# A planned single-core kernel (Fourier mixing beside 16-head attention): the planner's margin behind some loads is 3 instead of 5

## Chip, cores, metric

One core of one Trainium2 chip. The time is the device time of one execution in microseconds (us), the median over several runs.

## What is computed

Two independent layers on 2048 tokens of width 448, joined along the last axis. In float32 throughout:

```python
# A: Fourier mixing with given matrices
a = x @ dft_hid_re.T
b = x @ dft_hid_im.T
yA = dft_seq_re @ a - dft_seq_im @ b
# B: full softmax attention, 16 heads of 28
q, k, v = split(xB @ wqkv)
p = softmax(q @ k.T * 28**-0.5)
yB = (p @ v).reshape(2048, 448) @ wo
out = concat([yA, yB], axis=-1)
```

## The kernel before

**Attention** fills most of the time. Scores are made transposed, 128 keys by 512 queries at a time: per head 16 key tiles times 4 query chunks, 1024 tiles in all. Each is one matmul on PE (L1302; L1243 for a head's first key tile) into a bank, then an exponential on ACT (L1310) into a buffer `kept`; every four matmuls of a key tile (L1285) then add values weighted by these into one bank per head. There are eight banks: one for filler work, seven for scores and sums. A head's first key tile goes a longer way: ACT copies it out (L1247), DVE transposes it and takes maxima (L1248, L1249, L1255, L1260, L1258), spreads the result over the query columns (transpose L1269), POOL or DVE puts it in as one more row of that head's queries (L1272), and adds it to the copied tile (L1274), which ACT exponentiates (L1276). No other score matmul of the head can start before its L1272.

**Fillers** are PE work that stands between the score matmuls: projections to queries, keys and values (L687, 512 or 224 columns) and the Fourier side (L877). A projection from column block 3 on needs a *weight piece*: 256 KB loaded on SP (L612) into a buffer `raw`, converted on ACT (L613) and its rest made on POOL (L616).

**Checks.** The Fourier side does not multiply by the whole 2048 x 2048 matrices. It uses their symmetries and checks them on all entries: pieces of both matrices go through six buffers `raw` (loads L928 and, of a mirrored copy, L966), are added or subtracted (L972, on DVE or POOL, whichever is free) and reduced to a maximum on DVE (L909). Token pieces (L821, L824) and folded weights (L584 to L587, converted on ACT at L589) use the same buffers.

**What sets the order.** Every engine has its own instruction order, and all of them come from a planner that runs when the kernel is built (`Schedule.run`, L237 on). It takes tasks with guessed durations, dependencies and due times (`key`) and plays the five engines forward in time: when an engine is free, it gets the ready task that is due first, and a task with a choice of engines goes to whichever of them comes first. The order in which tasks are handed out becomes the order of instructions; on the chip each instruction waits by semaphores for what it really needs. For a load the planner guesses a landing from a flow of 225 GB/s and a fixed time, and then adds the task's `slack` before it lets a consumer start:

```python
lat = max(landed[-len(t.dmas):]) - at + 0.1 + t.slack
```

`slack=SLACK` stands at the loads of matrix entries (`Stack.loads` L928, `Turned` L966, `Rows` L1045, `column_check` L1020, two loads in `special`), of token pieces (L821, L824), of folded weights (L584, L587) and of weight pieces (L612). Loads of keys and queries (L1181, L1182) have a margin of their own, `SLACK_K`, which is 2.5.

Of the kernel before, what the change touches and what calls it, by code (L numbers as in the profile page):

```python
# [36 lines left out]
LEAD = 6  # L37
NFILL = 1
V_OWN = 2
SLACK = 5.0  # L40
MIRROR_AT = 60.0, 110.0
FILL_AT = 48.0, 75.0
N_WARM = 9
# [311 lines left out]
def tile_kernel(ctx, tc, xa, wre, wim, wd, xb, wqkv, wo, out):  # L355
# [82 lines left out]
    def dma(key, emit, size=256, extra=0.0, n=1, **kw):  # L438

        return sch.add({"SP": 0.4}, key, lambda e: emit(), dmas=[(size, extra)] * n, **kw)  # L440
# [5 lines left out]
    def act(key, emit, d=ACT_P, **kw):  # L446
        return sch.add({"ACT": d}, key, lambda e: emit(), **kw)
# [4 lines left out]
    def pool(key, emit, d=POOL_2, **kw):  # L452
        return sch.add({"POOL": d}, key, lambda e: emit(), **kw)
# [125 lines left out]
    def load_folded(part, key, after):  # L579
# [3 lines left out]
        cols = slice(part * D, (part + 1) * D)  # L583
        lw = [dma(key, lambda: nc.sync.dma_start(w()[:, :, :E], wd[:, :2, part * D:part * D + E]), 226, slack=SLACK, use=[raws[2]])]  # L584
        ld = dma(key + 0.5, lambda: nc.sync.dma_start(n()[:, :, :D], wd[:, :2, cols]), 448, acq=[raws[0]])
        ld2 = dma(key + 0.7, lambda: nc.sync.dma_start(n2()[:, :, :D], wd[:, 2:, cols]), 448, acq=[raws[1]])
        ld3 = [dma(key + 1, lambda: nc.sync.dma_start(r()[:, :, :E], wt_d[:, :, part * D:part * D + E]), 226, slack=SLACK, deps=turned[0], use=[raws[3]])]  # L587
        f = lambda l: w_first.folded[:, part, :, l, :]
# [17 lines left out]
    class Piece:  # L606


        def __init__(self, src, key):
            self.hi, self.lo = whi.slot(), wlo.slot()  # L610
            raw = Square(raw_s.slot())
            ld = dma(key, lambda: nc.sync.dma_start(raw.t, src()), 256, slack=SLACK, acq=[raw])  # L612
            a = act(key + 1, lambda: nc.scalar.activation(self.hi.t, raw.t, AF.Copy), ACT_S, soon=SOON,  # L613
# [199 lines left out]
    def tokens(c, key, after):  # L813
# [6 lines left out]
        for q, st in enumerate((c, NH - 1 - c)):  # L820
            ln.append(dma(key + 0.3 * q, lambda q=q, st=st: nc.sync.dma_start(  # L821
                n.t[:, q].rearrange("p (b x) -> p b x", b=2), bass.AP(tensor=xa.tensor, offset=xa.offset + st * tile_x,
                ap=[[4 * P, P], [NH * tile_x, 2], [1, 2 * P]])), 256, slack=SLACK, use=[n]))
            lr.append(dma(key + 0.3 * q + 0.1, lambda q=q, st=st: nc.sync.dma_start(  # L824
                r.t[:, q].rearrange("p (b x) -> p b x", b=2), bass.AP(tensor=xt_d.tensor, offset=xt_d.offset + st * tile_x // 2,
                ap=[[2 * P, P], [NH * tile_x // 2, 2], [1, 2 * P]])), 256, slack=SLACK, deps=turned[1], use=[r]))
        z = [pool(key, lambda p=p, k=k: nc.gpsimd.memset(r.t.rearrange("p a (b k m) -> p (a b) k m", b=2, k=2)[p:p + 1, :, k], 0.0), 0.3, deps=lr, use=[r])
# [88 lines left out]
    def begun(key):  # L916
        return [opened[min(max(int((key - begins[0]) / P_H), 0), H - 1)]]

    class Stack:
# [6 lines left out]
        def loads(self, part, key, n, off, step):  # L926
            src, rows = (wre, wim)[part], P // n
            return [dma(key, lambda a=a: nc.sync.dma_start(self.t[a * rows:(a + 1) * rows], bass.AP(  # L928
                tensor=src.tensor, offset=src.offset + off(a), ap=[[step, rows], [1, H1]])), 512 / n, slack=SLACK, deps=begun(key), use=[self.raw]) for a in range(n)]

# [704 lines left out]
```

## Time and profile before

| | before |
|---|---|
| median of 3 runs | 695.8 us (695.61 to 695.81) |
| profiled execution | 693.96 us, its span 692.4 us |
| granted TensorE clock, mean | 0.998 |
| DMA, mean over the span | 190 GB/s |
| exponentials on ACT (L1310) | 960, 506.0 us busy |
| score matmuls (L1302) | 960, 295.7 us busy |
| value sums (L1285) | 2048, 246.2 us busy |

The profile is one execution. PE is TensorE's matmuls, PEld its weight loads, DVE VectorE, ACT ScalarE, POOL GpSimd, SP the engine that issues DMAs. A row of a group gives line, engine, operation, what is written and read, shapes and count, then busy time, mean duration in ns, and the idle time before it with what ended it. A row of the timeline begins with start and duration in us; idle time before it and what ended it stand in square brackets. The busy time of PE is modelled, as matmuls are pipelined.

### The profile page before, as it was taken

Reading aid. Unit: us, or ns where it says so; the run is one execution under the profiler, and the core shown is the slowest. Engines: PE = TensorE matmul, PEld = TensorE weight load, DVE = VectorE, ACT = ScalarE, POOL = GpSimd, SP = SyncE. Lnnn points to the kernel's source line nnn. Section 1 sums busy time; section 2 is a strip of 40 time slices with the busy share of each in tenths; the row PEclk is TensorE's granted clock in tenths of the full one; section 3 lists DMA queues with packets and bytes.
Section 4 is the critical chain, followed back from the end, with each engine's and each line's share of the span. In section 5 each row is a group of like instructions: output and inputs, shape, how many; then the busy total and the mean of one; then the engine's idle time right before and its main releaser. Section 6 shows DMA issues by size and latency. Waiting matters only on the chain. (4 is left out here: it accounts for less than half of the span.)

```text
span 692.4 us, 12770 instructions
## 1 busy us (share of the span) xinstructions
PE 683.0 (99%) x4147; PEld 395.3 (57%) x4147; DVE 491.8 (71%) x857; ACT 607.7 (88%) x1233; POOL 354.8 (51%) x344
## 2 busy tenths in 40 slices
PE   8999999999999999999999999999999999999996
PEld 7897555555555555455455545555555555455786
DVE  6458639587969489698978796989697927531780
ACT  6416999999998999999999999999999999999442
POOL 8504315357545346554735564548778421545660
PEclk9999999999999999999999999999999999999999
DMA  8866789886969888989779898671443311344177
GB/s 302 282 198 208 187 213 233 215 222 209 250 175 249 214 237 236 229 238 232 217 201 248 222 249 225 185 233 59 147 145 99 101 49 52 99 133 137 34 183 243
DMA packets 101808, 131.38 MB, mean 190 GB/s; under 512 B 34231, under 2 KB 64585, under 8 KB 101733
## 3 DMA queue, kind: packets, MB, share of 16 engines
q1 hardware_dynamic: 99685, 128.62, 67.7%
q0 software_dynamic: 2048, 1.86, 1.1%
q8 instruction: 35, 0.57, 0.4%
q14 instruction: 40, 0.33, 0.2%
HBM read 100.28 MB, written 36.88 MB: 198 GB/s over the span
## 5 line engine op out<-in xcount | busy, mean ns | idle before, releaser
L1310 ACT ACTIVATE kept<-bank 128x512 f32<-128x512 f32 x960 | 506.0, 708 | 13.0 <-PE bank L1302 11.9
L1302 PE MATMUL bank<-q,k 98*128 98x512 f32 x960 | 295.7, 410 | 1.5 <-ACT kept L1310 0.8
L1285 PE MATMUL bank<-kept,v 128*32 128x512 f32 x2048 | 246.2, 598 | 0.0
L1302 PEld LDWEIGHTS bank<-q,k 98*128 98x128 f32 x960 | 171.4, 188 | 129.9 <-ACT kept L1310 92.2
L972 POOL TENSOR_TENSOR raw<-raw,raw 128x1024 f32<-128x1024 f32 (+3 forms) x57 | 107.9, 1898 | 72.3 <-DVE raw L972 37.7
L1285 PEld LDWEIGHTS bank<-kept,v 128*32 128x32 f32 x2048 | 53.4, 109 | 116.5 <-issue 110.8
L909 DVE TENSOR_REDUCE far<-raw 128x1 f32<-128x1024 f32 (+3 forms) x78 | 86.0, 1111 | 8.2 <-POOL raw L1086 4.4
L1274 POOL TENSOR_TENSOR kept<-kept,mb 128x512 f32<-128x512 f32 x41 | 58.2, 1427 | 26.5 <-DVE mb L1269 13.9
L1247 ACT ACTIVATE kept<-bank 128x512 f32<-128x512 f32 x64 | 40.3, 693 | 24.7 <-PE bank L1243 21.6
L1272 POOL CAST q<-mb 1x512 fp32r<-1x512 f32 x31 | 24.6, 808 | 69.3 <-DVE mb L1269 49.2
L1248 DVE STREAM_TRANSPOSE mb<-bank 128x512 f32<-128x512 f32 x64 | 43.6, 700 | 20.0 <-PE bank L1243 15.0
L1348 POOL TENSOR_TENSOR kept<-kept 128x512 f32<-128x512 f32 x16 | 20.9, 1304 | 59.9 <-DVE kept L1343 42.7
L1276 ACT ACTIVATE kept<-kept 128x512 f32<-128x512 f32 x64 | 49.4, 783 | 0.0
L687 PE MATMUL bank<-big,whi 128*128 128x512 f32 x132 | 46.8, 396 | 0.0
L687 PE MATMUL bank<-wd,big 128*128 128x224 f32 x288 | 43.9, 274 | 0.4 <-ACT kept L1310 0.3
L687 PEld LDWEIGHTS bank<-wd,big 128*128 128x128 f32 x288 | 40.5, 191 | 4.7 <-issue 0.8
L1269 DVE STREAM_TRANSPOSE mb<-am 128x512 f32<-128x512 f32 x62 | 41.9, 696 | 0.8
L1249 DVE TENSOR_REDUCE qm<-mb 128x16 f32<-128x512 f32 x64 | 41.5, 668 | 0.4
L972 DVE TENSOR_TENSOR raw<-raw,raw 128x1024 f32<-128x1024 f32 (+3 forms) x27 | 34.5, 1281 | 6.5 <-DMA raw<-wre 6.3
L1339 DVE STREAM_TRANSPOSE kept<-kept 128x512 f32<-128x512 f32 x16 | 11.4, 710 | 27.6 <-ACT kept L1337 27.5
L797 DVE COPY kept<-bank 128x224 f32<-128x224 f32 x32 | 12.3, 386 | 24.1 <-PE bank L687 23.8
L1272 DVE CAST q<-mb 1x512 fp32r<-1x512 f32 x31 | 27.9, 902 | 1.0
(181 smaller groups left out, 782.6 us busy)
## 6 DMA issues: line engine op xcount, KB each, us to landing
raw<-wre SPq DMA_DIRECT2D x64, 256.0 KB
raw<-wim SPq DMA_DIRECT2D x64, 256.0 KB
qkd<-kept SPq DMA_DIRECT2D x40, 256.0 KB
k<-qkd SPq DMA_DIRECT2D x64, 112.0 KB
q<-qkd SPq DMA_DIRECT2D x64, 112.0 KB
kept<-xb SPq DMA_DIRECT2D x16, 256.0 KB
vd<-kept SPq DMA_DIRECT2D x8, 512.0 KB
raw<-wre SPq DMA_DIRECT2D x32, 128.0 KB
```

Of the source, the lines that this page charges most:

```text
L687: nc.tensor.matmul(o.t[:, :cols], w(), x(), start=(i == 0), stop=(i == n - 1))
L909: far_done.append(dve(key, lambda: nc.vector.tensor_reduce(far[rows, part, n:n + 1], t(), axis=AX.X if len(t().shape) == 2 else AX.XY, op= ...
L972: return sch.add(d, at, lambda g: eng[g].tensor_tensor(xv(), xv(), yv(), op=op), deps=[*x.ld, *y.ld, *deps], use=[x.raw, y.raw])
L1248: t = dve(key, lambda o=o, tm=tm: nc.vector.transpose(tm.t, o.t), 0.73, deps=[m], acq=[tm], use=[o], lock=[o], own=RAW_S)
L1249: rs.append(dve(key, lambda tm=tm, c=c: nc.vector.tensor_reduce(qm.t[:, 0, c * NT:(c + 1) * NT], tm.t.rearrange("p (j r) -> p j r", r=32), ...
L1269: t = dve(key, lambda mb=mb, c=c: nc.vector.transpose(mb.t, f32(am.t)[:, c * NT:(c + 1) * NT].unsqueeze(2).to_broadcast([P, NT, 32])), 0.7 ...
L1272: row.append(sch.add({"DVE": 0.95, "POOL": 0.8}, key, lambda e, q=q, mb=mb: eng[e].tensor_copy(q.t[96:97, :], mb.t[96:97, :]), deps=[t], u ...
L1274: sh = sch.add({"DVE": 1.15, "POOL": 1.4}, key + (6 if h == 0 else 0), lambda e, s=s, mb=mb: eng[e].tensor_tensor(s.t, s.t, mb.t, op=ALU.add),
L1276: shown.append(act(key, lambda s=s: nc.scalar.activation(s.t, s.t, AF.Exp, scale=SCALE), ACT_S, deps=[sh], use=[s.pair]))
L1285: nc.tensor.matmul(o.t[c * VW:(c + 1) * VW, :], VT[h].t[:, kt // 4, kt % 4, :], tiles[c].t, start=(kt == 0), stop=(kt == NT - 1))
L1302: m = pe(key, lambda e, o=o, q=q, kt=kt: nc.tensor.matmul(o.t, KT[h][kt // 4].t[:KM, kt % 4 * P:(kt % 4 + 1) * P], q.t[:KM, :], start=True ...
L1310: es[h, kt].append(act(key - 20, lambda o=o, p=p: nc.scalar.activation(p.t, o.t, AF.Exp, scale=SCALE), deps=[m], use=[o, p.pair]))
```

## The change

One number: what the planner adds behind the landings of the loads that carry `slack=SLACK`. The loads, the consumers and the waits stay the same; each engine's order is made anew with it.

```diff
 V_OWN = 2
-SLACK = 5.0
+SLACK = 3.0
 MIRROR_AT = 60.0, 110.0
```

The number of instructions on each engine changes hardly, their order in many places. Tasks that may go to DVE or POOL or ACT also change engines: 15 checks of 128x1024 stand on DVE instead of 13 and 17 on POOL instead of 19, 8 of 128x8 on DVE instead of 4 and 8 on POOL instead of 12, and one of the four 128x256 token conversions moves from ACT to DVE. Three places follow (`bank_122` is the filler bank, `raw` the six load buffers).

**The first weight piece, on ACT and SP** (where head 3's scores end and head 4's begin, heads counted from 0). On ACT before, around the fourth exponential L1276 of head 4's first tile:

```order
L1310 ACTIVATE kept_101<-bank_126 128x512
L1310 ACTIVATE kept_101<-bank_129 128x512
L1310 ACTIVATE kept_106<-bank_127 128x512
L1310 ACTIVATE kept_106<-bank_124 128x512
L1276 ACTIVATE kept_109<-kept_109 128x512
L1310 ACTIVATE kept_104<-bank_128 128x512
L613 ACTIVATE whi<-raw_73 128x512
L1310 ACTIVATE kept_104<-bank_125 128x512
```

And now:

```order
L613 ACTIVATE whi<-raw_73 128x512
L1310 ACTIVATE kept_100<-bank_127 128x512
L1310 ACTIVATE kept_100<-bank_126 128x512
L1310 ACTIVATE kept_107<-bank_125 128x512
L1310 ACTIVATE kept_107<-bank_124 128x512
L1310 ACTIVATE kept_103<-bank_123 128x512
L1310 ACTIVATE kept_103<-bank_128 128x512
L1310 ACTIVATE kept_101<-bank_127 128x512
L1310 ACTIVATE kept_101<-bank_126 128x512
L1276 ACTIVATE kept_109<-kept_109 128x512
```

The conversion L613 stood two places behind that L1276 and stands nine places ahead of it; counted from the start of ACT's order it is 10 places earlier. The other three pieces move up by 30, 6 and 6 places, the second folded weight (L589) by 37 and the first by 8. On SP before, around the load of the same piece:

```order
L928 DMA raw_71<-wre 64x1024 x2
L928 DMA raw_75<-wre 64x1024 x2
L1181 DMA k_86<-qkd 56x1x512
L1182 DMA k_86<-qkd 28x512
L928 DMA raw_74<-wre 64x1024 x2
L1181 DMA k_88<-qkd 56x1x512
L1182 DMA k_88<-qkd 28x512
L928 DMA raw_72<-wre 64x1024 x2
L612 DMA raw_73<-wqkv 128x4x128
```

And now:

```order
L928 DMA raw_71<-wre 64x1024 x2
L928 DMA raw_72<-wre 64x1024 x2
L928 DMA raw_75<-wre 64x1024 x2
L928 DMA raw_74<-wre 64x1024 x2
L1181 DMA k_86<-qkd 56x1x512
L1182 DMA k_86<-qkd 28x512
L928 DMA raw_71<-wre 64x1024 x2
L612 DMA raw_73<-wqkv 128x4x128
L1181 DMA k_88<-qkd 56x1x512
```

The piece is issued two DMAs earlier, and now ahead of the key load into `k_88` instead of behind it. The other three move up by 13, 0 and 2 DMAs; ahead of the third, four loads of matrix entries have moved from behind the key load into `k_85` to in front of it.

**A head's query rows, on DVE** (head 3, its last three transposes L1269). Before:

```order
L1269 STREAM_TRANSPOSE mb_117<-am_120 128x512
L1272 CAST q_95<-mb_116 1x512
L1274 TENSOR_TENSOR kept_111<-kept_111,mb_116 128x512
L909 TENSOR_REDUCE far<-raw_71 128x1
L1274 TENSOR_TENSOR kept_111<-kept_111,mb_117 128x512
L1269 STREAM_TRANSPOSE mb_116<-am_120 128x512
L909 TENSOR_REDUCE far<-raw_75 128x1
L1272 CAST q_98<-mb_116 1x512
L909 TENSOR_REDUCE far<-raw_73 128x1
L1274 TENSOR_TENSOR kept_114<-kept_114,mb_116 128x512
L1269 STREAM_TRANSPOSE mb_117<-am_120 128x512
```

And now:

```order
L1269 STREAM_TRANSPOSE mb_117<-am_120 128x512
L909 TENSOR_REDUCE far<-raw_71 128x1
L1272 CAST q_95<-mb_116 1x512
L972 TENSOR_TENSOR raw_75<-raw_75 128x8
L909 TENSOR_REDUCE far<-raw_75 128x1
L1274 TENSOR_TENSOR kept_102<-kept_102,mb_117 128x512
L1269 STREAM_TRANSPOSE mb_116<-am_120 128x512
L1272 CAST q_98<-mb_116 1x512
L909 TENSOR_REDUCE far<-raw_73 128x1
L972 TENSOR_TENSOR raw_70<-raw_70,raw_74 128x512
L1269 STREAM_TRANSPOSE mb_117<-am_120 128x512
```

Two checks L972 have come to DVE here; the second, which reads two loads, stands directly in front of the last transpose. Over the 15 heads from the second on, the checks, Fourier steps and reductions that stand on DVE between a head's first L1248 and its last L1269 are 57 instead of 84.

**Fillers, on PE** (within head 1's scores). Before:

```order
L1302 MATMUL bank_126<-q_95,k_85 128x512
L1302 MATMUL bank_125<-q_96,k_85 128x512
L687 MATMUL bank_122<-wd,big 128x224 x6
L1302 MATMUL bank_128<-q_98,k_85 128x512
L687 MATMUL bank_122<-wd,big 128x224 x3
L1302 MATMUL bank_124<-q_99,k_85 128x512
L687 MATMUL bank_122<-wd,x_69 128x224 x2
L1302 MATMUL bank_126<-q_95,k_85 128x512
L1302 MATMUL bank_127<-q_96,k_85 128x512
L1285 MATMUL bank_123<-kept_108,v_91 32x512 x2
```

And now:

```order
L1302 MATMUL bank_126<-q_95,k_85 128x512
L687 MATMUL bank_122<-wd,big 128x224 x4
L1302 MATMUL bank_125<-q_96,k_85 128x512
L687 MATMUL bank_122<-wd,big 128x224 x2
L1302 MATMUL bank_128<-q_98,k_85 128x512
L1302 MATMUL bank_127<-q_99,k_85 128x512
L1302 MATMUL bank_124<-q_95,k_85 128x512
L687 MATMUL bank_122<-wd,big 128x224 x2
L1302 MATMUL bank_126<-q_96,k_85 128x512
L1285 MATMUL bank_123<-kept_108,v_91 32x512 x2
```

Eleven fillers stood ahead of the value sums (L1285) here, and eight do now; the other three come behind.

## The prediction

> **What bounds the kernel now.** I read the page first (busy times, slices, chain), then the busy times by stage, then who waited for whom, then single rows. The page's own verdict misleads here: its chain of waits ends at one closing output copy and says nothing of the middle, and PE looks full.
>
> ```profile
> PE 683.0 (99%) x4147; PEld 395.3 (57%) x4147; DVE 491.8 (71%) x857; ACT 607.7 (88%) x1233; POOL 354.8 (51%) x344
> ```
>
> By stage (us, then PE, PEld, DVE, ACT and POOL busy), ACT is the engine with no room between 70 and 640 us; only in the last 52 us is it far from full.
>
> ```profile
> 70.00:100.00 30.00, 30.00 (x188) 15.18 (x191) 13.01 (x25) 30.00 (x62) 8.00 (x7) 1.00 0.88 212
> 100.00:600.00 500.00, 498.91 (x3027) 259.64 (x3020) 397.61 (x627) 486.18 (x982) 273.68 (x235) 1.00 0.71 189
> 600.00:640.00 40.00, 39.55 (x257) 21.84 (x261) 9.14 (x22) 38.72 (x86) 17.91 (x26) 1.00 0.46 139
> 640.00:692.40 52.40, 46.81 (x267) 39.98 (x266) 28.30 (x67) 20.06 (x50) 22.59 (x26) 0.98 0.56 152
> ```
>
> That PE is not the bound shows in the waits of 100 to 600 us (total, times, longest). Its weight loads stood 78.4 us behind ACT, which had not yet freed a bank, while ACT stood only 8.9 us behind the score matmuls and 12.6 us in all. The first row is PE's side, the rest are all that ACT has.
>
> ```profile
> PEld bank L1302 <- ACT kept L1310: 78.4, 120, 0.8
> ...
> ACT kept L1310 <- PE bank L1302: 8.9, 18, 1.0
> ACT kept L1247 <- DVE mb L1248: 1.5, 3, 0.9
> ACT kept L1247 <- PE bank L1243: 1.4, 4, 0.5
> ACT kept L709 <- PE bank L687: 0.6, 1, 0.6
> ACT wd L709 <- PE bank L687: 0.2, 1, 0.2
> ```
>
> So the stage lasts as long as ACT's own work (486.2 of 500 us) plus 13.8 us in which it stands. An order that changes nothing in ACT's work can win at most 13.8 us here, and loses whatever it adds to that.
>
> **The change part by part.** SLACK is no work and no wait of the chip. It is what the planner adds to its guess of a landing before it lets a consumer into the order, so every consumer of matrix entries, token pieces and weight pieces may now stand 2 us earlier in its engine's order, and its buffer comes free 2 us earlier. Nothing moves before about 105 us, and in the last 52 us ACT, and PE but for rows that are never reached, keep their order. The terms lie between.
>
> *The checks on DVE and POOL.* With the margin of 5 they did already run into their loads (DVE and POOL against DMA):
>
> ```profile
> DVE raw L972 <- DMA raw<-wre: 6.3, 1, 6.3
> ...
> POOL raw L972 <- DMA raw<-wre: 18.9, 7, 6.0
> POOL raw L972 <- DMA raw<-wim: 9.6, 5, 2.7
> ```
>
> At 2 us less, more of them will stand, and stand longer: 13 waits now, and 2 us on each of, say, twice as many is some 50 us at most, over two engines that have 102 us (DVE) and 226 us (POOL) free between 100 and 600. That is off the path as long as nobody needed by PE or ACT is queued behind; the rival below is the case in which somebody is. By the order, two 128x1024 and four 128x8 checks also go from POOL to DVE. The rows for DVE, then POOL:
>
> ```profile
> L972 DVE TENSOR_TENSOR raw<-raw,raw 128x1024 f32<-128x1024 f32 x16 | 23.7, 1483 | 6.4 <-DMA raw<-wre 6.3
> L972 DVE TENSOR_TENSOR raw<-raw,raw 128x8 f32<-128x8 f32 x3 | 2.3, 754 | 0.0
> L972 DVE TENSOR_TENSOR raw<-raw 128x8 f32<-128x8 f32 x1 | 1.8, 1751 | 0.0
> ...
> L972 POOL TENSOR_TENSOR raw<-raw,raw 128x1024 f32<-128x1024 f32 x24 | 58.8, 2449 | 28.6 <-DMA raw<-wre 15.9 <-DMA raw<-wim 7.4 <-DMA q<-qkd 4.4
> ```
>
> DVE gains 2 x 1.48 + 4 x 0.75 = 6.0 us of work, POOL loses more; on ACT this is 0. The Trainium skill, page "SBUF — State Buffer", section "Who interferes with whom", speaks against such a move: a DVE instruction with two SBUF inputs and a POOL one that reads SBUF lock each other out for a whole instruction. A check of 8 columns that took 1.75 us where its like took 0.75 fits that. By the rule the six could cost up to 6 x 2.45 = 14.7 us on DVE in place of 6.0, still inside its 102 us.
>
> *One conversion leaves ACT.* One of the four 128x256 token conversions moves from ACT to DVE.
>
> ```profile
> L462 ACT ACTIVATE big<-raw 128x256 fp32r<-128x256 f32 x4 | 2.0, 593 | 0.0
> ```
>
> 2.0 us for four is 0.5 us off ACT, and DVE there has room: **-0.5 us**, bounded by 0 and -0.6.
>
> *The weight pieces.* Here a consumer stands in ACT's own queue. Four pieces (256 KB each) are issued at L612 and converted at L613; the rows give each issue and the conversion.
>
> ```profile
> 194.31 0.60 SPq L612 DMA_DIRECT2D raw<-wqkv  x1
> ...
> 279.99 0.60 SPq L612 DMA_DIRECT2D raw<-wqkv  x1
> ...
> 344.54 0.61 SPq L612 DMA_DIRECT2D raw<-wqkv  x1
> ...
> 415.67 0.60 SPq L612 DMA_DIRECT2D raw<-wqkv  x1
> ```
>
> ```profile
> 202.66 0.63 ACT L613 ACTIVATE whi<-raw 128x512 fp32r<-128x512 f32 x1
> ...
> 289.32 0.63 ACT L613 ACTIVATE whi<-raw 128x512 fp32r<-128x512 f32 x1
> ...
> 352.06 0.74 ACT L613 ACTIVATE whi<-raw 128x512 fp32r<-128x512 f32 x1
> ...
> 423.66 0.92 ACT L613 ACTIVATE whi<-raw 128x512 fp32r<-128x512 f32 x1
> ```
>
> How long such a load flies I take from loads of the same size that were waited for: four issues begin at 75.22 us, the last ends at 79.91, and the check that needs them starts at 84.24; four begin at 107.14, and the check that needs the first two starts at 112.43.
>
> ```profile
> 75.22 4.69 SPq L928 DMA_DIRECT2D raw<-wre  x4
> ...
> 84.24 1.23 DVE L972 TENSOR_TENSOR raw<-raw,raw 128x1024 f32<-128x1024 f32 x1 [6.25 <-DMA raw<-wre]
> ...
> 107.14 2.40 SPq L928 DMA_DIRECT2D raw<-wre  x4
> ...
> 112.43 2.39 POOL L972 TENSOR_TENSOR raw<-raw,raw 128x1024 f32<-128x1024 f32 x1 [6.04 <-DMA raw<-wre]
> ```
>
> So between 4.3 and 5.3 us; I take 5. The time from landing to conversion is then 3.3, 4.3, 2.5 and 3.0 us. By the order, the conversions move up 10, 30, 6 and 6 places on ACT. A place is 4.03 / 8 = 0.50 us:
>
> ```profile
> 182.81 4.03 ACT L1310 ACTIVATE kept<-bank 128x512 f32<-128x512 f32 x8 [0.50 <-PE bank L1302]
> ```
>
> That makes 5.0, 15.1, 3.0 and 3.0 us earlier. The issues move up 2, 13, 0 and 2 places on SP, an estimated 1.2, 9.8, 0 and 1.6 us. What is left is -0.5, -1.0, -0.5 and +1.6 us: at worst ACT stands 0.5 + 1.0 + 0.5 = 2.0 us, and with the flight at 5.3 us 2.9 us. On the other side, the first issue now stands ahead of the key load that SP could issue only at 191.51 us,
>
> ```profile
> 191.51 0.88 SPq L1181 DMA_DIRECT2D k<-qkd  x1
> ```
>
> and the third has four matrix loads moved out from between that key load and itself, so both should leave 2 to 3 us sooner than their places say. Then no conversion waits but the second: I take **+0.6 us**, between 0 and +2.9.
>
> *The fills on PE.* Filler matmuls (projections and transform) fall at other places between the score matmuls. At 113.00 us ACT stood 0.86 us because PE had 11 fillers and a run of sums in front of the next scores.
>
> ```profile
> 109.26 0.49 PE L687 MATMUL bank<-wd,big 128*128 128x224 f32 x3
> ...
> 113.00 1.58 ACT L1310 ACTIVATE kept<-bank 128x512 f32<-128x512 f32 x3 [0.86 <-PE bank L1302]
> ```
>
> Now 8 stand there, three fewer at 0.49 / 3 = 0.16 us at the most, so this wait shrinks by up to 0.5 us; but the three come later and may lengthen another. Over the whole stage the count of fillers done at any score matmul stays within about nine small ones of what it was, and back to equal again and again. A place redrawn gains or loses at random: I take **-0.4 us** here and 0 for the rest, with half of the 8.9 us either way as its bounds.
>
> Sum: -0.5 + 0.6 - 0.4 = -0.3 us against the profiled execution's 693.96 us (span 692.4, so 1.6 lie around it). The median of the runs, 695.8, is 1.8 above that, so the forecast is **695.5 us**.
>
> **The rivals.** *Fewer stalls, faster.* DVE chains from a first score tile to the next head's query row carry fewer checks in the new order, buffers free sooner, and fillers are spread better, so that half of the 8.9 us goes: 695.8 - 4.5 = 691.3 us. For it speaks the place at 113 us; against it that PE's order of scores is otherwise nearly the same. It decides once more than 1.4 us of the 8.9 are gone.
>
> *ACT waits for weight pieces, slower.* The three shortfalls above come true: 695.5 + 2.9 - 0.6 = 697.8 us. It decides if the pieces land over 5 us after their issue, or SP leaves no sooner than its places say.
>
> *A late landing in front of a head's query row, slower.* A check that waits for its load holds DVE, and behind it stands the transpose (L1269) that makes a query row for the next head. The head that opens at 164 us has its fourth row at 164.85, for a score matmul at 165.86:
>
> ```profile
> 164.24 0.61 POOL L1272 CAST q<-mb 1x512 fp32r<-1x512 f32 x1
> ...
> 165.86 0.87 PE L1302 MATMUL bank<-q,k 98*128 98x512 f32 x3
> ...
> 162.71 0.70 DVE L1269 STREAM_TRANSPOSE mb<-am 128x512 f32<-128x512 f32 x1
> ```
>
> Its slack is 1.0 us, and six banks of scores feed ACT for 6 x 0.50 = 3.0 us more; a wait over 4.0 us in front of that transpose goes to ACT. In the new order a check that reads two loads (128x512) now stands there. At the 6.0 us that POOL stood once, a head loses 2.0 us, and two such heads 4.0 us: 695.5 + 4.0 = 699.5 us. Against it: the 13 waits for loads above are 34.8 us in all, 2.7 us on average, under the 4.0 us that it takes.
>
> That the change does nothing is ruled out by the order; that it moves only idle is the forecast.
>
> **How the numbers follow.** A measurement of this kernel can tell about 0.2% (1.4 us) from no change. Forecast (694.4 to 697.2): 0.46. Fewer stalls: 0.25. Weight pieces: 0.15. Late landing at a head: 0.14. The range goes down to a third of the 8.9 us gone (695.8 - 3.0 = 692.8) and up to the last rival (699.5), which leaves out less than 2 in 10. Faster is the second case, slower the last two (0.29), same the first. The likeliest case's own range is 694.4 to 697.2.
>
> **What would show it.** Right: ACT busy in 100 to 600 us within 1 us of 486, its waits on L1302 between 7 and 11 us, more DMA waits on DVE and POOL, none on ACT. Wrong: a row "ACT whi L613 <- DMA raw<-wqkv" (the weight pieces); a wait of PE or ACT on L1272, L1269 or L1248 over 1 us (the head); or L1310's waits on L1302 under 6 us (fewer stalls).

## The result, and the profile after

The changed kernel takes 702.03 us (median of 4 runs, 700.29 to 705.76) against 695.79 us: ratio 1.0088, 95% interval [1.0061, 1.0115], **slower by 6.2 us** where 695.5 and no change were forecast. A second measurement beside other runs of the kernel before (margin_3 below) gave 1.0115 [1.0086, 1.0144]. The profiled execution is the slowest of the four: 705.76 us, span 704.1. One execution of the kernel before (750.74 us, granted clock 0.851) and one of both_mended (3767.32 us) are far above all others of the same kernel and are left out of every median and ratio below.

By stage (us, then PE, PEld, DVE, ACT and POOL busy, granted clock, DMA share, GB/s), the loss lies between 100 and 600 us and in the last stage:

```profile
...
100.00:600.00 500.00, 495.52 (x2992) 258.46 (x2995) 397.56 (x615) 480.74 (x970) 269.22 (x232) 1.00 0.70 187
...
640.00:704.10 64.10, 55.47 (x304) 44.49 (x302) 31.44 (x70) 26.73 (x64) 28.61 (x38) 0.95 0.47 124
```

ACT stands 19.3 us of the 500 instead of 13.8. Who waited for whom there (total, times, longest): all of ACT, then PE, then the checks on POOL and DVE against their loads.

```profile
ACT kept L1310 <- PE bank L1302: 12.2, 23, 1.8
ACT kept L1247 <- PE bank L1243: 4.6, 5, 3.0
ACT kept L709 <- PE bank L687: 0.6, 1, 0.6
...
PE bank L1243 <- DMA q<-qkd: 2.1, 2, 1.7
PE bank L1243 <- DVE mb L1248: 1.8, 1, 1.8
...
POOL raw L972 <- DMA raw<-wre: 18.8, 8, 7.2
POOL raw L972 <- DMA raw<-wim: 18.2, 4, 8.6
...
DVE raw L972 <- DMA raw<-wre: 9.6, 3, 5.3
...
DVE raw L972 <- DMA raw<-wim: 1.4, 2, 0.9
```

The waits of PE on L1243 are new. To find where time goes I followed ACT's exponentials: the start of the nth L1310 in one trace, less its start in the other. The changed kernel is 0.2 us *ahead* at the 191st (172.8 us before), 3.9 us behind at the 211th (184.7 us), 4.6 at the 621st, 7.2 at the 631st (436.4 and 442.1 us), 6.6 at the last. Two steps, 4.1 and 2.6 us, are all of it; the rest are steps of up to 1.4 us within ten exponentials, which cancel. Both stand at a head's first tiles (L1243 on PE, L1247 on ACT, L1248 on DVE).

**First place.** PE stands 1.74 us for a query load:

```profile
168.98 1.45 PE L1302 MATMUL bank<-q,k 98*128 98x512 f32 x5
172.17 0.60 PE L1243 MATMUL bank<-q,k 84*128 84x512 f32 x1 [1.74 <-DMA q<-qkd]
172.56 0.60 PE L687 MATMUL bank<-wd,big 128*128 128x224 f32 x2
172.96 0.66 PE L1302 MATMUL bank<-q,k 98*128 98x512 f32 x1
173.42 1.67 PE L687 MATMUL bank<-wd,big 128*128 128x224 f32 x7
175.01 2.27 PE L1285 MATMUL bank<-kept,v 128*32 128x512 f32 x16
177.22 0.50 PE L1243 MATMUL bank<-q,k 84*128 84x512 f32 x1
```

SP issued it only after nine loads for checks (L966, L928). The rows of SP, after and then before, where it left 5.8 us sooner, behind three of them:

```profile
163.25 1.71 SPq L966 DMA_DIRECT2D raw<-mirror  x4
165.06 2.39 SPq L928 DMA_DIRECT2D raw<-wre  x5
167.54 0.52 SPq L1181 DMA_DIRECT2D q<-qkd  x1
```

```profile
160.39 1.30 SPq L966 DMA_DIRECT2D raw<-mirror  x3
161.78 0.36 SPq L1181 DMA_DIRECT2D q<-qkd  x1
```

From 172.4 us PE then has half its clock for 3.4 us (the granted clock is the third number from the right); no other stretch of the scores in this trace is below 1.00. ACT waits 3.01 us for the second L1243, which stands behind nine fillers and sixteen value sums in the new order.

```profile
165.00:172.40 7.40, 5.66 (x33) 2.86 (x33) 3.70 (x6) 7.40 (x17) 6.29 (x5) 1.00 0.95 233
172.40:175.80 3.40, 3.40 (x15) 2.42 (x18) 3.33 (x6) 2.16 (x5) 0.00 (x0) 0.50 0.91 190
```

DVE also stood 3.15 us in a check whose load had not landed, ahead of the head's first L1248. On the rows this cost PE nothing here: between 165 and 190 us the wait for q is PE's only one.

```profile
170.26 1.98 DVE L972 TENSOR_TENSOR raw<-raw,raw 128x512 f32<-128x512 f32 x1 [3.15 <-DMA raw<-wre]
172.17 2.33 DVE L909 TENSOR_REDUCE far<-raw 128x1 f32<-128x1024 f32 x2
...
176.53 0.71 DVE L1248 STREAM_TRANSPOSE mb<-bank 128x512 f32<-128x512 f32 x1
```

**Second place.** On DVE six checks now stand ahead of a head's first L1248; in the kernel before, that transpose came first and the checks between it and the next ones. After, then before:

```profile
435.94 2.04 DVE L972 TENSOR_TENSOR raw<-raw,raw 128x512 f32<-128x512 f32 x1
438.01 1.65 DVE L1023 TENSOR_TENSOR raw<-raw 1x512 f32<-1x512 f32 x1
439.70 2.77 DVE L909 TENSOR_REDUCE far<-raw 1x1 f32<-1x512 f32 x4
442.40 0.69 DVE L1248 STREAM_TRANSPOSE mb<-bank 128x512 f32<-128x512 f32 x1
```

```profile
427.33 0.72 DVE L1248 STREAM_TRANSPOSE mb<-bank 128x512 f32<-128x512 f32 x1 [1.53 <-PE bank L1243]
...
436.16 0.68 DVE L1023 TENSOR_TENSOR raw<-raw 1x512 f32<-1x512 f32 x1
...
438.17 0.67 DVE L972 TENSOR_TENSOR raw<-raw,raw 128x512 f32<-128x512 f32 x1
```

L1248 is what frees a bank that ACT has long copied, and PE's next first-tile matmul waits for it; PE stands, and with it the scores behind:

```profile
443.15 0.50 PE L1243 MATMUL bank<-q,k 84*128 84x512 f32 x1 [1.76 <-DVE mb L1248]
```

The last stage is 64.1 us here, but part of it is the lag, and its own length moves without any change of order: from the start of the last L1310 to the end of the span it is 49.4 us in the trace of before, 54.6 here, 51.6 in margin_3, and 52.2 in queries_late, whose order there is that of before. I give it no share.

### The profile page after: what moved, and what is told of

Its sections match the earlier page's. It is cut to its first block, busy times and chain, and to the rows that moved or that the text cites. A ratio compares the mean times of both kernels' runs of the same rounds, so it can differ in the third digit from the quotient of the medians.

```text
span 704.1 us, 12776 instructions
## 1 busy us (share of the span) xinstructions
PE 687.7 (98%) x4147; PEld 398.0 (57%) x4147; DVE 499.5 (71%) x856; ACT 607.6 (86%) x1232; POOL 354.7 (50%) x346
## 5 line engine op out<-in xcount | busy, mean ns | idle before, releaser
L1310 ACT ACTIVATE kept<-bank 128x512 f32<-128x512 f32 x960 | 508.2, 721 | 16.7 <-PE bank L1302 15.3
L1302 PE MATMUL bank<-q,k 98*128 98x512 f32 x960 | 297.4, 410 | 1.5 <-ACT kept L1310 1.4
L1285 PE MATMUL bank<-kept,v 128*32 128x512 f32 x2048 | 246.6, 599 | 0.0
L1302 PEld LDWEIGHTS bank<-q,k 98*128 98x128 f32 x960 | 171.5, 188 | 130.5 <-ACT kept L1310 91.0
L972 POOL TENSOR_TENSOR raw<-raw,raw 128x1024 f32<-128x1024 f32 (+3 forms) x52 | 101.6, 1957 | 93.2 <-DVE raw L972 31.6
L1285 PEld LDWEIGHTS bank<-kept,v 128*32 128x32 f32 x2048 | 53.4, 109 | 116.1 <-issue 110.7
L1274 POOL TENSOR_TENSOR kept<-kept,mb 128x512 f32<-128x512 f32 x41 | 57.6, 1417 | 13.5 <-DVE mb L1269 10.8
L1247 ACT ACTIVATE kept<-bank 128x512 f32<-128x512 f32 x64 | 40.5, 711 | 26.5 <-PE bank L1243 24.8
L1248 DVE STREAM_TRANSPOSE mb<-bank 128x512 f32<-128x512 f32 x64 | 43.4, 699 | 13.7 <-ACT kept L1247 8.7
L972 DVE TENSOR_TENSOR raw<-raw,raw 128x1024 f32<-128x1024 f32 (+3 forms) x32 | 39.1, 1223 | 19.4 <-DMA raw<-wre 17.7
L1276 ACT ACTIVATE kept<-kept 128x512 f32<-128x512 f32 x64 | 50.9, 808 | 0.0
L1272 POOL CAST q<-mb 1x512 fp32r<-1x512 f32 x31 | 23.4, 761 | 52.3 <-DVE mb L1269 40.7
L687 PEld LDWEIGHTS bank<-wd,big 128*128 128x128 f32 x288 | 42.0, 195 | 4.6 <-issue 0.8
L1269 DVE STREAM_TRANSPOSE mb<-am 128x512 f32<-128x512 f32 x62 | 42.0, 696 | 0.7
L1249 DVE TENSOR_REDUCE qm<-mb 128x16 f32<-128x512 f32 x64 | 41.2, 666 | 0.3
L1272 DVE CAST q<-mb 1x512 fp32r<-1x512 f32 x31 | 30.8, 999 | 1.0
L1243 PE MATMUL bank<-q,k 84*128 84x512 f32 x64 | 27.1, 429 | 3.8 <-DMA q<-qkd 2.1
L710 DVE TENSOR_TENSOR kept<-bank,kept 128x512 fp32r<-128x512 f32 x20 | 13.3, 685 | 20.9 <-ACT kept L709 20.7
```

Of the source, the lines that this page charges most:

```text
L687: nc.tensor.matmul(o.t[:, :cols], w(), x(), start=(i == 0), stop=(i == n - 1))
L972: return sch.add(d, at, lambda g: eng[g].tensor_tensor(xv(), xv(), yv(), op=op), deps=[*x.ld, *y.ld, *deps], use=[x.raw, y.raw])
L1248: t = dve(key, lambda o=o, tm=tm: nc.vector.transpose(tm.t, o.t), 0.73, deps=[m], acq=[tm], use=[o], lock=[o], own=RAW_S)
L1249: rs.append(dve(key, lambda tm=tm, c=c: nc.vector.tensor_reduce(qm.t[:, 0, c * NT:(c + 1) * NT], tm.t.rearrange("p (j r) -> p j r", r=32), ...
L1269: t = dve(key, lambda mb=mb, c=c: nc.vector.transpose(mb.t, f32(am.t)[:, c * NT:(c + 1) * NT].unsqueeze(2).to_broadcast([P, NT, 32])), 0.7 ...
L1272: row.append(sch.add({"DVE": 0.95, "POOL": 0.8}, key, lambda e, q=q, mb=mb: eng[e].tensor_copy(q.t[96:97, :], mb.t[96:97, :]), deps=[t], u ...
```

## The experiments

Theories: **two places** (the loss is these two steps; undone, it comes back); **DVE** (at the first place a check that waits in front of L1248 is what costs, the queries don't matter); **spread-out** (a margin too small costs at every head, and a mend only moves the wait).

To change one place and nothing else, most kernels let the planner write its whole order into a list, move named instructions in that list, and issue it:

```
-                t.emit(e)
+                plan.append((t, e))
...
+    for e, n, to in MOVES:
+        own = [x for x in plan if x[1] == e]
+        x, y = own[n], own[to]
+        plan.remove(x)
+        plan.insert(plan.index(y) + (to > n), x)
+    for t, e in plan:
+        t.emit(e)
```

So `("DVE", 486, 480)` makes DVE's task 486 its 480th, and a repeated move carries several. The table gives every run: medians, its ratio to the kernel before on the same chip with 95% interval, and from its trace ACT's lag behind the trace of before: the steps at the first place (191st to 211th exponential), just behind it (to the 241st, 202.2 us), at the second place (621st to 631st), and the lag at the last.

| kernel | us | before | ratio | 1st place | behind it | 2nd place | last |
|---|---|---|---|---|---|---|---|
| after | 702.03 | 695.79 | 1.0088 [1.0061, 1.0115] | 4.1 | 0.4 | 2.6 | 6.6 |
| queries_first | 708.66 | 696.63 | 1.0166 [1.0129, 1.0204] | 8.2 | 0.5 | 4.2 | 11.7 |
| place_one | 705.46 | 696.63 | 1.0125 [1.0085, 1.0165] | 5.8 | 0.5 | 4.0 | 8.7 |
| place_one_two | 703.79 | 696.63 | 1.0096 [1.0061, 1.0130] | 6.5 | 0.4 | 0.7 | 7.6 |
| queries_late | 699.50 | 696.63 | 1.0037 [1.0008, 1.0066] | (1.9) | 0.0 | 0.0 | 2.1 |
| checks_later | 709.01 | 695.94 | 1.0166 [1.0134, 1.0198] | 8.6 | 0.5 | 4.2 | 11.6 |
| both_places | 708.06 | 695.94 | 1.0173 [1.0146, 1.0199] | 9.0 | 0.4 | 0.7 | 9.5 |
| tiles_first | 700.12 | 696.52 | 1.0056 [1.0033, 1.0079] | 0.6 | 1.4 | 0.7 | 2.6 |
| matrix_only | 701.88 | 695.94 | 1.0080 [1.0053, 1.0106] | 1.7 | 0.4 | 4.2 | 4.6 |
| pieces_only | 698.89 | 695.94 | 1.0042 [1.0023, 1.0061] | 0.0 | -0.2 | 0.0 | 2.7 |
| margin_2 | 707.20 | 696.52 | 1.0124 [1.0078, 1.0170] | 0.1 | 0.1 | 3.6 | 11.5 |
| margin_4 | 701.56 | 696.52 | 1.0065 [1.0042, 1.0089] | 5.1 | 0.4 | 0.0 | 5.3 |
| margin_8 | 712.24 | 696.52 | 1.0208 [1.0165, 1.0251] | 0.8 | 0.2 | -0.8 | 16.0 |
| margin_3 | 704.34 | 697.11 | 1.0115 [1.0086, 1.0144] | 4.3 | 0.4 | 2.6 | 5.9 |
| first_mended | 704.05 | 697.11 | 1.0085 [1.0057, 1.0112] | 0.7 | 4.8 | 2.6 | 8.3 |
| second_mended | 701.31 | 697.11 | 1.0061 [1.0037, 1.0084] | 4.8 | 0.5 | 0.7 | 7.8 |
| both_mended | 701.44 | 697.11 | 1.0057 [1.0032, 1.0081] | 0.9 | 2.2 | 0.7 | 5.2 |

(In queries_late the step comes just ahead of the 191st.)

**queries_first.** SP's order at the first place as in the kernel before: four query loads and a key load ahead of seven matrix loads.

```
+MOVES = (("SP", 161, 167),) * 5 + (("SP", 163, 172),) * 7
```

> The changed kernel with one edit of SP's order: the query and key loads (L1181/L1182) for the first tiles at 172 us stand ahead of seven matrix loads (L928), as they do in the kernel before. Two-places theory: the 1.74 us wait of L1243 and the half clock behind it go, 3 to 4.4 us of the 6.2 come back, 697.6 to 699.0 us. Spread-out theory (late checks cost a little at every head, and a repair only moves the wait): 701 to 703 us. DVE theory (the check at 170.26 us that stood 3.15 us in front of L1248 is what costs): 701 us or more, since the check stays where it is and its load leaves later.

708.66 us, slower than the change alone. The wait for q is gone (L1243 at 169.88 us, no idle), but the check's load now leaves later, the check stands 6.96 us, L1248 comes at 179.34, and PE stands 5.12 us. On DVE, then on PE:

```profile
173.04 2.01 DVE L972 TENSOR_TENSOR raw<-raw,raw 128x512 f32<-128x512 f32 x1 [6.96 <-DMA raw<-wre]
...
179.34 1.30 DVE L1248 STREAM_TRANSPOSE mb<-bank 128x512 f32<-128x512 f32 x2
```

```profile
180.10 1.22 PE L1302 MATMUL bank<-q,k 98*128 98x512 f32 x2 [5.12 <-DVE mb L1248]
```

Of what was expected only the DVE theory's "701 us or more" holds. With its load that late, the check in front of L1248 costs more than the late queries did; this is the price of the mend, not of the change, in whose trace nothing on PE waits for that transpose.

**place_one, place_one_two.** The same, and the check with two reductions behind the head's first L1248; the second kernel also moves the first L1248 at the second place ahead of its six checks.

```
+MOVES = (("SP", 161, 167),) * 5 + (("SP", 163, 172),) * 7 + (("DVE", 176, 185),) * 3
```

```
+MOVES = (("SP", 161, 167),) * 5 + (("SP", 163, 172),) * 7 + (("DVE", 176, 185),) * 3 + (("DVE", 486, 480),)
```

> As queries_first, and on DVE the 128x512 check and two reductions go behind the first L1248 of that head. Two-places theory: no wait left at 172 us, all 4.4 us come back, 697.2 to 698.2 us. DVE theory: the same 697.2 to 698.2 here, but not in queries_first. Spread-out theory: 701 to 703 us.

> As place_one, and at 435 to 442 us the first L1248 of the later head stands ahead of the six checks (L972, L1023, L909) on DVE. Two-places theory: another 2.0 to 2.6 us, 694.8 to 696.2 us, the time of the kernel before. Spread-out theory: 701 to 703 us. If only the first place counts: 697.2 to 698.2 us.

At the first place both miss: the checks now stand in front of the *second* L1248, and PE waits for that one.

```profile
178.85 0.80 PE L1302 MATMUL bank<-q,k 98*128 98x512 f32 x1 [3.26 <-DVE mb L1248]
```

At the second place one moved instruction takes the step from 4.0 us (place_one, with half clock behind; 2.6 without, in the changed kernel) to 0.7.

**queries_late.** The kernel before, margin 5 throughout, with SP's order at that place as in the changed kernel.

```
+MOVES = (("SP", 160, 170),) * 2 + (("SP", 161, 172),) * 3
```

> The kernel before, margin 5 throughout, with that one piece of SP's order as in the changed kernel: the query and key loads behind the matrix loads. Two-places theory: L1243 waits for q at about 170 us, 1.5 to 4.4 us slower, 697.3 to 700.2 us. DVE or spread-out theory: no check is moved, so within 0.7 us of 695.8.

1.0037 (2.9 us by the medians), lag 1.9 us: the late queries alone cost this (L1243 waits 1.61 us), with no half clock behind. So DVE is not the only cause. What half clock adds shows at the second place: 2.6 us without it (after, margin_3, first_mended), 4.0 to 4.2 us with it (queries_first, place_one, checks_later, matrix_only). The queries and 1.4 to 1.6 us of half clock make 3.3 to 3.5 of the 4.1 us, an estimate; what the rest is, the nine fillers for one, was not tried.

**checks_later, both_places.** The check and its two reductions behind the first two L1248 and L1249, with SP as in the changed kernel; then with the queries first and the second place mended as well.

```
+MOVES = (("DVE", 176, 190),) * 3
```

```
+MOVES = (("SP", 161, 167),) * 5 + (("SP", 163, 172),) * 7 + (("DVE", 176, 190),) * 3 + (("DVE", 486, 480),)
```

> The changed kernel with one edit of DVE's order: the 128x512 check and the two reductions of the first place stand behind the first two L1248 and L1249 of that head, not ahead of them; SP's order stays, so the queries are late still. DVE theory (what costs at the first place is a check that waits for its load in front of L1248, whose bank PE needs): the lag of ACT between 172 and 185 us falls from 4.4 to the 1.8 us that late queries alone cost in queries_late, 699 to 700 us. Query theory (late queries and the half clock behind them): the lag stays at 3.5 to 4.4 us, 701 to 702 us.

> As checks_later, with the queries ahead of the matrix loads on SP as in queries_first, and with the first L1248 of the later head ahead of its six checks. If the loss lies at the two places and each needs what is undone here: no wait of over 1 us at either, the lag of ACT at the end of the scores between -1 and +1.5 us against the kernel before, 694.5 to 697.5 us. If a repair only moves the wait: 700 us or more.

Both are far over what a mended place was to give, by 7 us and more, and in one way: the checks now stand in front of the *third* L1248. checks_later speaks against both of its theories (699 to 700 and 701 to 702 us); both_places comes out as its last sentence has it (700 us or more, a wait that moved). In both_places the reduction of v there (L1212) also waits for its load, which SP issues at 173.78 us (at 170.85 in the kernel before), and PE pays for both:

```profile
179.72 0.69 DVE L1212 TENSOR_REDUCE ok<-v 128x1 f32<-128x512 f32 x1 [2.70 <-DMA v<-vd]
180.32 1.49 DVE L972 TENSOR_TENSOR raw<-raw,raw 128x512 f32<-128x512 f32 x1
181.74 2.33 DVE L909 TENSOR_REDUCE far<-raw 128x1 f32<-128x1024 f32 x2
183.99 1.30 DVE L1248 STREAM_TRANSPOSE mb<-bank 128x512 f32<-128x512 f32 x2
```

```profile
184.75 1.22 PE L1302 MATMUL bank<-q,k 98*128 98x512 f32 x2 [5.23 <-DVE mb L1248]
```

What follows, from four kernels that moved the checks behind one or two of the four L1248: what stands on DVE between them, and above all what waits for a load there, can come onto PE's path. It need not: in the kernel before, a check and a reduction stand in front of this head's third L1248 (L972 at 175.30 us for 0.91 us), and PE waits for nothing from 165 to 180 us.

**tiles_first.** So all four L1248 go first, then the check, its reductions and L1212; the six matrix loads into the checks' buffers are ordered behind them.

```
+MOVES = (("SP", 161, 167),) * 5 + (("SP", 163, 172),) * 7 + (("DVE", 486, 480),)
+BEHIND = tuple(("SP", n, "DVE", 192) for n in (188, 187, 186, 185, 184, 183))
+BEHIND += (("DVE", 190, "DVE", 192), ("DVE", 178, "DVE", 191), ("DVE", 177, "DVE", 190), ("DVE", 176, "DVE", 189))
...
+    for e, n, f, to in BEHIND:
+        x = [x for x in plan if x[1] == e][n]
+        y = [x for x in plan if x[1] == f][to]
+        plan.remove(x)
+        plan.insert(plan.index(y) + 1, x)
```

> As both_places, and at the first place all four L1248 of the head stand ahead of the check, its two reductions and the reduction of v (L1212) on DVE; the six matrix loads whose buffers the checks hold are ordered behind them. If what costs is any instruction on DVE that waits for a load between a head's four L1248: no wait of PE over 1 us at either place, ACT's lag at the end of the scores 0 to 2 us, 695 to 698.5 us. If a repair only moves the wait (to matrix loads that now leave later, or to a query row): 700 us or more.

Both steps are gone (0.6 and 0.7 us), and these are all of PE's waits from 100 to 640 us:

```profile
PE bank L1302 <- ACT kept L1310: 1.5, 4, 0.5
PE bank L1302 <- DVE mb L1248: 0.6, 1, 0.6
PE bank L1302 <- POOL q L1272: 0.2, 1, 0.2
```

The check that had stood for its load runs in 0.65 us without a wait:

```profile
178.72 1.31 DVE L1248 STREAM_TRANSPOSE mb<-bank 128x512 f32<-128x512 f32 x2 [1.14 <-ACT kept L1247]
179.96 0.65 DVE L972 TENSOR_TENSOR raw<-raw,raw 128x512 f32<-128x512 f32 x1
```

But the median, 700.12 us, is 1.6 over the range expected and 3.6 over the kernel before; the time is the one forecast for a wait that only moves (700 us or more), though PE has no long wait left.

**matrix_only, pieces_only.** Margin 3 for one class of loads, 5 for the other (L928, L966, L1020, L1045, L1080 are matrix entries; L584, L587, L612, L821, L824 the rest). The edit in matrix_only, shown at L1020 and the same at its other four loads:

```
-SLACK = 5.0
+SLACK = 5.0; SLACK_M = 3.0
...
-                     slack=SLACK, deps=[col_stored[part, ps]], use=[raw])
+                     slack=SLACK_M, deps=[col_stored[part, ps]], use=[raw])
```

> Margin 3 for landings of matrix entries alone, 5 for token pieces and weights. If the margin as such costs (checks that stand in front of a head's first tile): 698 to 704 us, with at least one L1243 or L1302 that waits over 1 us for a L1248. If the two places are an accident of one order: within 1.5 us of the kernel before, 695 to 698 us.

> Margin 3 for token pieces and weights alone, 5 for matrix entries. If only late checks cost: within 1.5 us of the kernel before, 695 to 698 us. If any redrawn order of this kernel falls into such places: 698 us or more, again with a wait of PE for L1248 or for q.

Matrix entries alone give 1.0080, the whole change but for the noise, with a wait of 1.00 us for q at the first place and the second place as it was (PE waits 1.76 us for L1248, and here half clock follows). Token and weight pieces alone give 1.0042 with no such step: PE's one wait for L1248 is 1.0 us, and the 2.7 us come in steps of 1.3 us and less. A redrawn order costs something even without the two places.

**margin_2, margin_4, margin_8.** Line 40 alone.

```
-SLACK = 5.0
+SLACK = 4.0
```

> SLACK 4.0. If a smaller margin lets more waiting checks in front of the L1248, with a price per place: between the two kernels, 697 to 701 us. If each redrawn order meets such places by chance: anywhere from 695 to 705 us, with a wait of PE for L1248 or q at each step of ACT's lag over 1.5 us.

> SLACK 2.0. Price per place: three or more waits of PE over 1 us for L1248, 704 to 712 us. Chance: 695 to 705 us.

> SLACK 8.0. Price per place: no wait of PE over 1 us for L1248; if buffers freed 3 us later in the plan cost nothing, within 1.5 us of the kernel before, 694.5 to 697.5 us. Chance: 695 to 705 us.

4 gives 1.0065, in the range for chance: the first place is there (L1243 waits 2.25 us for q, half clock behind), the second is not. 2 gives 1.0124; its 707.20 us lie in the range for a price per place, but only one wait for L1248 is over 1 us (2.26 us at 448 us), not three. Among its other waits is one of PE for a query row, the step that my third rival priced:

```profile
321.45 0.93 PE L1302 MATMUL bank<-q,k 98*128 98x512 f32 x3 [2.69 <-DVE q L1272]
```

8 gives 1.0208, most of it behind 442 us, outside of both forecasts; PE has one idle over 1 us there (1.89 us at 468 us), and the many waits of ACT that make up the rest of its 16.0 us were not followed. So there is no price per us of margin: of 2, 3, 4, 5 and 8 only 5 shows no idle of PE over 1 us between 100 and 640 us.

**margin_3, first_mended, second_mended, both_mended.** The change, each place mended alone, and both (tiles_first again), on one chip. second_mended moves one instruction:

```
+MOVES = (("DVE", 486, 480),)
```

first_mended is tiles_first without that move.

> The changed kernel as it is. If the two places hold most of the loss: 6 to 8 us over the kernel before, with a wait of L1243 for q at about 170 us and one for L1248 at about 441 us, and half clock behind them in some runs.

> First place alone mended as in tiles_first. Two places: 3 to 4.5 us less than margin_3. Wait moved or loss elsewhere: within 1.5 us of margin_3.

> Second place alone mended: the first L1248 ahead of six checks on DVE, one instruction moved. Two places: 1.5 to 3.5 us less than margin_3. Otherwise within 1 us of it.

> The same kernel as tiles_first, for the comparison on one chip. If nothing else is lost: within 1.5 us of the kernel before. If small steps all along the new order cost as well: 2 to 5 us over it.

The second mend holds: 3.0 us by the medians, as forecast. (In its traced execution, 703.63 us, ACT's last lag is larger than in margin_3, by a wait for a weight piece at 355 us.) The first does not: 0.3 us by the medians where 3 to 4.5 were forecast. It takes its own step from 4.3 to 0.7 us and gives it back 10 to 20 us later: in first_mended ACT waits there for L1274 on POOL, then for a weight piece, and PE stands 1.93 us with half clock behind.

```profile
199.83 0.63 ACT L1276 ACTIVATE kept<-kept 128x512 f32<-128x512 f32 x1 [1.44 <-POOL kept L1274]
...
201.92 0.63 ACT L613 ACTIVATE whi<-raw 128x512 fp32r<-128x512 f32 x1 [0.48 <-DMA raw<-wqkv]
```

That fits the six matrix loads that leave later in this kernel, but it was not tried apart. With both mended 4.3 us by the medians stay over the kernel before (1.0057; 1.0056 in tiles_first), within the 2 to 5 us forecast for a new order that costs in small steps all along. So of the 7.2 us of margin_3 the two mends together give back 2.9, no more than the second alone. No kernel here beats the kernel before.

## Why the prediction was wrong, step by step

- **What bounds the kernel**: right. The stage still lasts as long as ACT's work plus what ACT stands; only that sum rose (idle 13.8 to 19.3 us).
- **The checks on DVE and POOL**: the bound held, the conclusion did not, and this is the step that failed. Between 100 and 600 us the waits of L972 for matrix entries rose from 27.2 us in 11 waits to 18.8 + 18.2 + 9.6 + 1.4 = 48.0 us in 17: 20.8 us more, inside the "some 50 us at most" that I allowed. I then put them "off the path as long as nobody needed by PE or ACT is queued behind" and looked for somebody behind them at one place only, a head's query rows (L1269, L1272), where I found 4.0 us of cover. The head's first tiles (L1243, L1247, L1248) come earlier and can have far less: the four L1248 free the banks that PE's next matmuls take. At the second place six checks, none of them in a wait for its load, held the first L1248 back; PE stood 1.76 us, ACT fell back 2.6 us, and moving that one instruction gives 3.0 us of the time back. I counted what stands between the first L1248 and the last L1269 and not what stands in front of the first L1248. At the first place a check waited 3.15 us in front of L1248, too, but there no matmul of the changed kernel waited for it.
- **Buffers that come free 2 us earlier**: I wrote it down and priced nothing, and this is what failed at the first place. In SP's new order the next matrix loads stand ahead of the next head's query loads, and the queries left 5.8 us later. Alone that is 1.9 us of lag (queries_late).
- **The clock**: not in the sum at all. 3.4 us at half clock are 1.7 us of PE's work at a moment when ACT has nothing in stock; at the second place its price is 1.4 to 1.6 us.
- **The conversion**: right. Three instead of four on ACT, 1.4 us where it was 2.0.

```profile
L462 ACT ACTIVATE big<-raw 128x256 fp32r<-128x256 f32 x3 | 1.4, 780 | 0.0
```

- **The weight pieces**: ACT waits for none in the two traces of the changed kernel, so +0.6 was 0 there. But second_mended has the same order as the changed kernel on every engine but DVE, and on DVE up to 435 us, and its trace has such a wait:

```profile
355.15 0.63 ACT L613 ACTIVATE whi<-raw 128x512 fp32r<-128x512 f32 x1 [1.57 <-DMA raw<-wqkv]
```

So this term comes and goes from run to run.

- **The fills**: right at the place shown, 0.52 us where it was 0.86; over the whole stage the waits on L1302 rose, from 8.9 to 12.2 us.

```profile
113.24 3.04 ACT L1310 ACTIVATE kept<-bank 128x512 f32<-128x512 f32 x6 [0.52 <-PE bank L1302]
```

That the lag at the 191st exponential was -0.2 us, close to the -0.3 of the sum, is a coincidence: ten exponentials earlier it was +1.1 us, and in margin_3 it is -0.8 at the 191st. What broke the forecast most is the first tiles of two heads of 16, which the order showed and which I did not read. Of the signs named as wrong, the wait of PE on L1248 over 1 us came; of those named as right, more waits for loads on DVE and POOL and none on ACT came, ACT's busy time (480.7, not 486) and its waits on L1302 (12.2, not 7 to 11) did not.

What stays open: the 4.3 us left with both places mended. The trace of both_mended has steps of 1.7, 1.3 and 1.6 us at other spots (at 196, 220 and 349 us on the clock of before; the last lag is 5.2 us). tiles_first, the same kernel, has 0.9 us at the first of these and a last lag of 2.6 us. And pieces_only shows 1.0042 without either place. That a new order costs in small steps all along is thus not ruled out, and no run here tells its share.

The second place has one more cause, argued from rows. DVE's L972 took 2.04 us there and L1023 1.65 us, beside L972 and L1023 on POOL:

```profile
435.89 1.53 POOL L972 TENSOR_TENSOR raw<-raw,raw 128x512 f32<-128x512 f32 x1
437.51 1.61 POOL L1023 TENSOR_TENSOR raw<-raw 1x512 f32<-1x512 f32 x1
```

In the kernel before the like took 0.67 and 0.68 us on DVE. That is 2.3 us, more than the 1.76 us that PE stood; no run moved POOL's checks alone. It agrees with the section of the Trainium skill that the prediction quoted ("SBUF — State Buffer", "Who interferes with whom"); there I had set it against DVE's idle time instead of against what is queued behind.

## What to carry to other kernels

Where a consumer of a load is let in earlier, list for each in-order queue what stands *behind* it at the tightest place, and price the wait there, not against the engine's idle time; transposes and copies that free a bank for PE come first in that list, then loads of the next stage behind buffers in the issuing queue. Here a mend that moved the waiting instruction behind one or two of several such transposes only moved the wait to the next. And the margin of this planner isn't a slope: 2, 3, 4 and 8 were all slower than 5, with stalls that differ from order to order, so an order is judged by its stalls and not by its setting.

## What the runs showed of the hardware

An idle of PE far below 3.4 us can halve its clock for the next 3.4 us. Between 100 and 640 us of all traces, idles of PE of 1.73 to 2.7 us were met by half clock, at the latest 4 us behind them, 12 times of 18, idles over 3 us 4 times of 4 (for 3.4 or 6.8 us), and shorter ones, of 0.9 to 1.61 us, once of 6. The same idle goes both ways: 1.76 us at 441 us in the changed kernel, and 1.76 us at 439 us in matrix_only (clock third from the right).

```profile
441.00:446.00 5.00, 3.24 (x20) 1.46 (x22) 4.94 (x9) 3.17 (x8) 1.96 (x3) 1.00 0.84 264
```

```profile
442.00:445.40 3.40, 3.40 (x17) 0.64 (x17) 3.40 (x7) 2.70 (x6) 1.59 (x2) 0.50 0.78 259
```

Within one trace the stretches begin whole multiples of 3.41 us apart (after: 172.4, 680.9, 701.4 us, that is 149 and 6 of them). What decides is how much of an idle falls into one such window. With each trace cut into windows of 3.413 us on the grid of its own changes of clock, 16 windows that began between 100 and 640 us at full clock held 1.73 us of idle or more, and behind 15 of them the clock was half; of all full-clock windows with less, that came behind two (1.49 and 1.18 us). The 1.76 us of the changed kernel fell into two windows, 0.61 and 1.14 us; those of matrix_only fell into one. The Trainium skill, page "TensorE: Matmul & The Clock Gate", section "Part 1: The HAM clock gate", tells of a free-running window of 3413 ns, and these spacings agree; it gives at least one idle window of about 3.4 us as the condition for half clock, and here about half of that was enough.

The wait of DVE for POOL shows over all traces. A check L972 of 128x512 took 0.67 to 0.73 us on DVE where POOL did nothing (38 times). Where POOL's own L972 had begun first, it took the time to the end of that one and 0.54 to 0.59 us more (65 times of 65, up to 2.66 us). Where DVE had begun first, by 0.02 to 0.41 us, it took 0.65 to 0.72 us (12 times).
